# Three load buffers moved by 128 bytes in a decode step of attention plus a bilinear GLU

## The chip, the cores and the metric

The kernel runs on one core of a Trainium2 chip. The metric is the device time of one execution in microseconds (us). A core has TensorE (PE, matrix products), VectorE (DVE), ScalarE (ACT), GpSimd (POOL) and a queue engine (SP) that here issues all transfers; sixteen DMA engines carry them. The on-chip memory SBUF has 128 partitions, and a tile takes the same bytes in each of them. Place, in this document, means the byte within a partition at which a tile begins.

## The reference

One decode step for two sequences (B = 2), model width 512. The normalised input feeds an attention over the last 2048 positions of a cache with 32 heads of 128, and a gated product without a nonlinearity; both are added to the input. All values are 32-bit floats.

```python
xn = layernorm(x)                                   # x: (2, 1, 512)
q = (xn @ wq) as 32 heads of 128
k, v = k_cache[:, :, 6144:, :], v_cache[:, :, 6144:, :]      # W = max(256, 8192 // 4) = 2048
p = softmax(einsum("bhqd,bhkd->bhqk", q, k) * 128 ** -0.5)
A = einsum("bhqk,bhkd->bhqd", p, v) as (2, 1, 4096) @ wo
Bb = ((xn @ w_gate) * (xn @ w_up)) @ w_down         # hidden width 1376
return x + A + Bb
```

Nearly all bytes are those of k and v: 2 x 32 heads x 2048 x 128 x 4 bytes x 2 = 134 MB of the 159.5 MB that the kernel reads.

## The kernel before

**The stream.** The host lays all operands out in one array, `stream`, in the order in which they are used. `blocks()` (line 44) lists it as fields: for a head h, `("k", h, 4096)` and `("v", h, 4096)` floats in each partition, with slices of `wq` and `wo` of 512 floats beside them, and the weights of the GLU. Fields are grouped by three units of up to 4608 floats, so that a group fits one load buffer of `STEP` = 13,824 floats (55,296 bytes) in each partition.

**The loads.** `pump()` (lines 141 to 162) issues them on SP, each as one DMA of 128 contiguous rows, one for each partition. The first block (`x`, small selection matrices and a part of `wq`, 551 floats a partition) goes into a constant tile named `first`. All others go into three buffers, the pool `steps` (line 126): a buffer is taken when one is free, and `done()` (line 164) gives it back when the last of its fields has been used, and calls `pump()` again. There are 29 loads into these buffers: 16 of 55,296 bytes a partition, the others shorter; the last groups are cut into several loads of 2,048 to 18,432 bytes a partition so that the end of the stream can be used piece by piece.

**The work.** For each head, VectorE multiplies k in place by the broadcast q (`products`, line 272) and sums each product over the 128 of a row (`sums`, line 280). `maxima` and `weights` make the softmax with GpSimd's reductions across partitions and ScalarE's exponentials. TensorE weighs v by p (`weigh`, line 324), three heads behind k, brings the result into columns (`transpose`) and multiplies by `wo` (`project_o`). The GLU is done between the first heads. The order of the work on each engine is that of the text (`InOrder`, line 81, chains each instruction to the one before on its engine).

**Places.** The pools lie one behind the other in a partition: 16,512 bytes that are taken before the kernel's first tile, then the pool `const`, then `steps`, then `small`. In a pool tiles follow each other in the order in which they are first asked for, each rounded up to 32 bytes. The tiles of `const` are: `first` 2,204 bytes (2,208), `x_nat` 512, `mean_w` 512, `eps_t` 4 (32), six `p` of 512, four `oT` of 36 (64), `st`, `xc`, `sq` and `xn` of 32, `xnb` 4,096, `hT` 432 (448), `hX` 108 (128), `acc_sb` 2,048, `o_out` 512. That is 13,952, so `first` begins at 16,512 and the three buffers at 30,464, 85,760 and 141,056.

| tile | begins at byte | in units of 256 |
|---|---|---|
| `first` | 16,512 | 64.5 |
| load buffers | 30,464; 85,760; 141,056 | 119; 335; 551 |
| `s` (first of `small`) | 196,352 | 767 |

Every field of a load buffer is a multiple of 256 bytes wide (the narrowest are `wr` with 1,536 and the slices of `wq`, `wo` and `wd` with 2,048), so each field begins where its buffer does, modulo 256.

Of the kernel before, what the change touches and what calls it, by code (L numbers as in the profile page):

```python
# [8 lines left out]
F32 = mybir.dt.float32  # L9
# [7 lines left out]
P = 128  # L17
# [26 lines left out]
def blocks():  # L44

    def wd(n):
        return [("wd", i, D) for i in range(*WD[n])]

    def k(h):
        return [("k", h, CK)] + ([("wq", h, CP)] if h + HG < H else [])

    def v(h):
        return [("v", h, CK), ("wo", h, CO)]  # L60

    def gu(half):
        n = NC * (FH[half][1] - FH[half][0])
        return [("wg", half, n), ("wu", half, n)]

    units = []
    for h in range(LAG, H - 1):
        units += [k(h), v(h - LAG)]
    ones = [("pick", 0, 8 * B), ("rows", 0, NFB * B), ("carry", 0, M)]
    first = [("x", 0, B * NC)] + ones + [("w", 0, NC * DH)]  # L70
    loads = [[("w", 1, CQ - NC * DH)] + k(0) + k(1), gu(0) + k(2)]
    loads += [gu(1) + units[0] + units[1] + wd(0) + [("wr", 0, NS * P)]]
    loads += [sum(units[i : i + 3], []) for i in range(2, len(units), 3)]
    loads += [k(H - 1) + v(H - 1 - LAG) + wd(1)]
    out = [(("f", 0), first)] + [(("s", i), fields) for i, fields in enumerate(loads)]
    late, last = ("s", len(loads)), ("s", len(loads) + 1)
    out += [(late, v(H - 3)), (late, v(H - 2)), (last, [("v0", H - 1, CL)])]
    out += [(last, [("v1", H - 1, CK - CL)]), (last, [("wo", H - 1, CO)] + wd(2))]
    return out + [(last, wd(n)) for n in range(3, len(WD))]
# [33 lines left out]
def kernel(  # L113
# [11 lines left out]
    const = ctx.enter_context(tc.tile_pool(name="const", bufs=1))  # L125
# [3 lines left out]
    ps_c = ctx.enter_context(tc.tile_pool(name="ps_c", bufs=1, space=bass.MemoryType.PSUM))  # L129


    todo, at = [], 0
    for key, fields in blocks():
        todo.append((key, fields, at))
# [479 lines left out]
```

## Time and profile before

| | us |
|---|---|
| median of 3 runs (377.3 to 377.55) | 377.4 |
| the profiled execution | 377.5 |
| its span, first to last instruction | 375.7 |
| mean granted TensorE clock in it | 0.805 |

The page of the profile gives the busy time of each engine as a share of the span, then the span in 40 equal slices (a digit is the busy share in tenths; the row DMA is the mean over the sixteen DMA engines), then the DMA queues, and the chain of work that ended last. In the view of windows the last two columns are the DMA share and the GB/s moved. In the view of the DMA queues a packet is one row of a load, and the share is that of the sixteen engines' time in the window. In the view of waits the three numbers are the sum in us, how often, and the longest. In a tile's view the three durations are the least, the median and the greatest in ns. Nearly all instructions are recorded under line 97, the line of the helper that chains them, so tiles tell them apart.

### The profile page before, as it was taken

The numbers are of one execution on the slowest core, as the hardware profiler recorded it, in microseconds if no ns is written. First come the engines' busy times: TensorE is split into PE (matmuls) and PEld (weight loads), VectorE is DVE, ScalarE is ACT, GpSimd is POOL, SyncE is SP. The second block draws the span as 40 slices with busy tenths as digits, with TensorE's granted clock in tenths as the row PEclk, the third lists the DMA queues.
The fourth block names the chain that finished last, engine by engine and source line by source line (L and its number), as shares of the span: only waits on it lengthen the run. The fifth ranks groups of instructions, "written<-read, shape, count | busy, mean of one in ns | idle before, by whom it ended". The sixth has DMA issues, their size and how long they took to land.

```text
span 375.7 us, 2858 instructions
## 1 busy us (share of the span) xinstructions
PE 254.2 (68%) x1084; PEld 88.5 (24%) x1084; DVE 294.1 (78%) x146; ACT 58.6 (16%) x259; POOL 25.3 (7%) x78
## 2 busy tenths in 40 slices
PE   3496497886547486854858476685846669637996
PEld 3241023331112122211212121231212122212334
DVE  3299691998599499769949976994996799599950
ACT  1021001122021111201112020211202011211131
POOL 1001000000000000100000100000000000000010
PEclk9998967998697666888768696885869676857999
DMA  8999999899999999999999999999999999999995
GB/s 346 445 436 454 426 408 471 383 465 449 395 466 406 442 455 400 459 418 436 460 400 449 424 430 459 402 442 430 430 459 406 437 444 436 419 431 443 398 421 221
DMA packets 4492, 159.70 MB, mean 425 GB/s; under 512 B 512, under 2 KB 640, under 8 KB 1152
## 3 DMA queue, kind: packets, MB, share of 16 engines
q1 hardware_dynamic: 4480, 159.54, 98.5%
q8 instruction: 8, 0.13, 0.1%
q14 instruction: 4, 0.03, 0.0%
HBM read 159.48 MB, written 0.06 MB: 425 GB/s over the span
## 4 chain that ended last, share of the span: by engine, by line
DMA 63%; DVE 26%; PE 8%; ACT 1%; issue 0%; SPq 0%; DVEq 0%
DMA step<-in_stream_dram 63%; DVE s L97 13%; DVE step L97 13%; PE o_ps L97 3%; PE q L97 2%; PE acc L97 2%; PE tr L97 1%; ACT o_sb L97 0%; DVE m L97 0%; ACT oT L97 0%; SPq L97 0%; DVE rec L97 0%; DVE o_out L97 0%; DVEq L97 0%
## 5 line engine op out<-in xcount | busy, mean ns | idle before, releaser
L97 DVE TENSOR_TENSOR step<-step,q 128x4096 f32<-128x4096 f32 x31 | 136.6, 4407 | 52.4 <-DMA step<-in_stream_dram 52.4
L97 PE MATMUL q<-step,xnb 128*128 128x512 f32 (+1 forms) x128 | 92.4, 872 | 76.4 <-DMA step<-in_stream_dram 76.4
L97 DVE TENSOR_REDUCE s<-step 128x32 f32<-128x4096 f32 x32 | 141.4, 4419 | 1.1
L97 PE MATMUL o_ps<-step,p 128*16 128x512 f32 x512 | 68.9, 672 | 11.5 <-DMA step<-in_stream_dram 11.5
L97 PEld LDWEIGHTS q<-step,xnb 128*128 128x128 f32 x128 | 32.3, 275 | 130.5 <-DMA step<-in_stream_dram 77.5
L97 PE MATMUL acc<-step,oT 128*9 128x512 f32 (+1 forms) x88 | 35.4, 552 | 9.3 <-ACT oT L97 8.1
L97 PE MATMUL tr<-first,o_sb 128*128 128x2 f32 (+2 forms) x198 | 28.1, 261 | 15.4 <-ACT o_sb L97 13.0
L97 ACT COPY o_sb<-o_ps 128x512 f32<-128x512 f32 (+1 forms) x25 | 14.1, 568 | 140.7 <-PE o_ps L97 140.7
L97 PEld LDWEIGHTS tr<-first,o_sb 128*128 128x128 f32 x198 | 26.0, 200 | 36.8 <-ACT o_sb L97 32.4
L290 POOL PARTITION_ALL_REDUCE mm<-m x32 | 11.3, 354 | 283.1 <-DVE rec L97 180.1
L97 PEld LDWEIGHTS o_ps<-step,p 128*16 128x16 f32 x512 | 13.4, 104 | 69.9 <-issue 54.4
L97 ACT ACTIVATE nm<-mm 128x2 f32<-128x2 f32 x32 | 6.5, 203 | 131.4 <-POOL mm L290 131.4
L97 ACT ACTIVATE p<-s,nm 128x16 f32<-128x16 f32 x64 | 19.2, 300 | 1.0
L97 ACT ACTIVATE oT<-tr,rec 128x1 f32<-128x1 f32 x64 | 12.2, 260 | 28.5 <-PE tr L97 28.5
L306 POOL PARTITION_ALL_REDUCE sum<-rs x32 | 12.7, 398 | 55.0 <-ACT p L97 55.0
L97 PE MATMUL o_ps<-step,xn 128*2 128x512 f32 (+1 forms) x48 | 13.9, 616 | 0.0
L97 ACT ACTIVATION_READ_ACCUMULATOR p<-s,nm 128x1 f32 x64 | 12.0, 187 | 0.0
L97 DVE TENSOR_TENSOR step<-step,tr 128x4096 f32<-128x4096 f32 x1 | 4.4, 4422 | 9.3 <-DMA step<-in_stream_dram 9.3
L97 PEld LDWEIGHTS acc<-step,oT 128*9 128x9 f32 x88 | 4.5, 91 | 19.4 <-ACT oT L97 12.7
L97 PE MATMUL q<-xnb,mean_w 128*128 128x512 f32 (+2 forms) x18 | 8.3, 551 | 0.0
L97 DVE TENSOR_TENSOR o_out<-acc,x_nat 128x128 f32<-128x128 f32 x1 | 0.3, 292 | 8.8 <-PE acc L97 8.8
L97 DVE TENSOR_REDUCE m<-s 128x2 f32<-128x32 f32 x32 | 5.9, 186 | 1.1
(39 smaller groups left out, 40.5 us busy)
## 6 DMA issues: line engine op xcount, KB each, us to landing
step<-in_stream_dram SPq DMA_DIRECT2D x16, 6912.0 KB, 31.1
step<-in_stream_dram SPq DMA_DIRECT2D x2, 6400.0 KB, 32.8
step<-in_stream_dram SPq DMA_DIRECT2D x1, 6720.0 KB, 45.4
step<-in_stream_dram SPq DMA_DIRECT2D x1, 6656.0 KB, 29.0
step<-in_stream_dram SPq DMA_DIRECT2D x1, 5376.0 KB, 15.3
step<-in_stream_dram SPq DMA_DIRECT2D x1, 4864.0 KB, 29.6
step<-in_stream_dram SPq DMA_DIRECT2D x2, 2304.0 KB, 17.1
step<-in_stream_dram SPq DMA_DIRECT2D x1, 1536.0 KB, 14.6
```

The costliest lines, as they stand in the source:

```text
L97: made = call(*args, **kwargs)
L290: nc.gpsimd.partition_all_reduce(mm, m, P, bass_isa.ReduceOp.max)
L306: nc.gpsimd.partition_all_reduce(sum_t[h], rs, P, bass_isa.ReduceOp.add)
```

## The change

A tile of 32 floats in each partition, 128 bytes, is asked for in the pool `const` before any other. Nothing writes or reads it.

```diff
     ps_c = ctx.enter_context(tc.tile_pool(name="ps_c", bufs=1, space=bass.MemoryType.PSUM))
 
 
+
+    const.tile([P, 32], F32, name="place")
     todo, at = [], 0
     for key, fields in blocks():
```

All tiles of `const` behind it, the three load buffers and the tiles of `small` begin 128 bytes later: `first` at 16,640 (65 x 256), the buffers at 30,592, 85,888 and 141,184 (119.5, 335.5 and 551.5 x 256). The size of a buffer, the loads, their order and all instructions stay.

## The prediction

> **What bounds the kernel now.** I read the page from the top: busy times, the slices, the DMA queues, the chain that ended last. Then the windows of two stretches, the waits of VectorE and of the load queue, and the view of the DMA queues in three short windows.
>
> ```profile
> span 375.7 us, 2858 instructions
> ...
> PE 254.2 (68%) x1084; PEld 88.5 (24%) x1084; DVE 294.1 (78%) x146; ACT 58.6 (16%) x259; POOL 25.3 (7%) x78
> ...
> DMA  8999999899999999999999999999999999999995
> ...
> q1 hardware_dynamic: 4480, 159.54, 98.5%
> ...
> DMA 63%; DVE 26%; PE 8%; ACT 1%; issue 0%; SPq 0%; DVEq 0%
> ```
>
> No engine is busy for more than 78% of the span, but the queue that carries the loads keeps all sixteen DMA engines at work for 98.5% of it; the idle rest is the first slice and the last. The chain names loads for 63% and VectorE for 26%. That share of VectorE needs a second look, since work on the chain need not be what limits:
>
> ```profile
> core 0: us, PE busy (x) PEld busy (x) DVE busy (x) ACT busy (x) POOL busy (x), PEclk, DMA share, GB/s
> 100.00:200.00 100.00, 65.69 (x252) 20.31 (x255) 83.49 (x37) 14.95 (x69) 6.77 (x18) 0.76 1.00 434
> 1.70:372.10 370.40, 253.43 (x1072) 88.26 (x1076) 292.99 (x142) 57.60 (x259) 24.16 (x67) 0.80 1.00 431
> ```
>
> ```profile
> DVE step L97 <- DMA step<-in_stream_dram: 61.7, 11, 9.3
> ...
> SPq L97 <- DVE s L97: 309.8, 21, 31.4
> ```
>
> In the middle of the run (100 to 200 us) the DMA engines have no idle time (share 1.00, 434 GB/s) while VectorE rests for 16.5 us in 100 and waits for loads 61.7 us in all. The load queue (SP) in turn waits for VectorE's sums 309.8 us, but that is a queue waiting for a free buffer with its two earlier loads still under way:
>
> ```profile
> step<-in_stream_dram SPq DMA_DIRECT2D x16, 6912.0 KB, 31.1
> ```
>
> A load of 6912 KB (7.08 MB) takes 16.3 us at 434 GB/s and lands 31.1 us after its issue. So it stands 31.1 - 16.3 = 14.8 us behind the load ahead of it, and an issue that came late by less than that would leave no hole in the stream. Where the stream begins and ends, two windows in slices show, 0 to 3 us (75 ns a slice) and 371 to 372.4 us (35 ns a slice):
>
> ```profile
> GB/s 0 0 0 0 0 0 0 0 0 0 0 0 0 0 0 0 0 0 0 0 0 0 29 147 59 118 88 147 206 147 147 235 323 323 353 441 2014 3102 147 1809
> ```
>
> ```profile
> GB/s 351 293 176 176 176 468 117 59 351 176 176 117 293 176 234 234 176 176 176 117 117 234 117 117 59 59 117 0 0 59 0 0 0 0 0 0 0 0 0 0
> ```
>
> The first bytes move after 22 empty slices, at 1.7 us, the last in the 30th slice, at 372.05. The time is therefore: start (1.7 us), 370.4 us of unbroken stream, and 3.6 us for what follows the last bytes.
>
> **The change, part by part.** It adds no instruction: a tile that nothing writes or reads has no memset, no DMA and no wait. It removes none, and the order on each engine and on each queue (SP's and GpSimd's among them) is that of before. What moves is places. From the tile sizes the constants end and the first load buffer begins at byte 30,464 of a partition, which is 119 x 256; a buffer is 55,296 = 216 x 256 bytes, so all three begin on even multiples of 128, and every field in them is a multiple of 256 wide. With 128 bytes ahead the buffers begin at 119.5 x 256, and every row of every one of their 29 loads starts and ends in the middle of a 256-byte piece. The constants and the small tiles move by 128 as well.
>
> *Term 1: the rows of the loads.* A load writes 128 rows, one in each partition, and sixteen engines share them: 29 x 128 / 16 = 232 rows on each engine. What a row costs follows from two windows. In the last loads the rows are 2,048 bytes; the long loads' rows are 55,296 bytes:
>
> ```profile
> DMA packets 51, 0.09 MB, mean 188 GB/s; under 512 B 6, under 2 KB 6, under 8 KB 51
> ...
> q1 hardware_dynamic: 51, 0.09, 48.9%
> ```
>
> ```profile
> DMA packets 883, 43.39 MB, mean 434 GB/s; under 512 B 96, under 2 KB 96, under 8 KB 96
> ...
> q1 hardware_dynamic: 880, 43.35, 100.2%
> ```
>
> The first (371.3 to 371.8 us) moves 188 GB/s in 48.9% of its time, so 384.5 GB/s while busy, or 16 x 2048 / 384.5 = 85.2 ns for a row. The second (100 to 200 us) gives 434 / 1.002 = 433.1 GB/s, or 2042.8 ns for a row. The difference over 53,248 bytes is 0.0368 ns a byte: 4.7 ns for 128 bytes, 9.4 ns for 256, and 85.2 - 75.3 = 9.9 ns for a row whatever its length.
>
> Is a start on an odd multiple of 128 dearer? The trace of before has one load of that sort. The tile `first` begins at 16,512 = 64.5 x 256, and its 128 rows of 2,204 bytes are the first on the engines. Here are two windows in which nothing else moves, 2.3 to 2.7 us and 2.4 to 2.6 us:
>
> ```profile
> DMA packets 58, 0.13 MB, mean 320 GB/s; under 512 B 0, under 2 KB 0, under 8 KB 58
> ...
> q1 hardware_dynamic: 58, 0.13, 83.0%
> ```
>
> ```profile
> DMA packets 31, 0.07 MB, mean 342 GB/s; under 512 B 0, under 2 KB 0, under 8 KB 31
> ...
> q1 hardware_dynamic: 31, 0.07, 90.2%
> ```
>
> While busy: 320 / 0.830 = 385.5 GB/s and 342 / 0.902 = 379.2. By the fit an undisturbed row of 2,204 bytes takes 9.9 + 81.0 = 90.9 ns, which is 387.9 GB/s. With 128 bytes' time more it would be 368.9, with 256 bytes' more 351.6. The two readings lie by the first of these, 0.6% and 2.2% under it. So I take 0 for this term. Its ends: upward, one more 256-byte piece on each row, 232 x 9.4 = 2.2 us, as the cost that belongs to a row's two ends; and where a cost goes with the bytes, the lower reading's 2.2% of 370.4 us = 8.3 us. Downward, what the even places could be costing now is at most the fixed 9.9 ns of a row, 232 x 9.9 = 2.3 us: nothing else in a stream at share 1.00 can be won, because bytes over the steady rate is all that is left. The zero is nearest to the rows of `first`, which have the place in question; their weakness is that they are short, few, and run while the stream is only starting.
>
> [...]
>
> *Term 2: VectorE and TensorE on the moved buffers.* Both read the buffers, VectorE writes its products back into them, and all these operands now start 128 bytes on.
>
> ```profile
> L97 DVE TENSOR_TENSOR step<-step,q x31: 4398/4400/4422, 25.6 to 352.4; 128x4096 f32<-128x4096 f32 x31
> ...
> L97 PE MATMUL o_ps<-step,p x512: 592/592/1062, 62.8 to 368.6; 128*16 128x512 f32 x171
> ```
>
> The 31 products take 4398 to 4422 ns in whichever of the three buffers, on all the field offsets that occur. No row shows them on an odd multiple of 128; I take 0. This would be covered in any case up to a point: VectorE has 83.49 us of work in the 100, so its work could grow by a fifth before it took the place of the loads. TensorE at 65.69 has more room. Without that cover, 1% on VectorE's 294.1 us would cost 2.9 us. The ends of this term are therefore 0 and 0, except in the tail after the last bytes, where a few matmuls read the buffer: below 0.1 us.
>
> *Term 3: the moved small tiles and constants.*
>
> ```profile
> first<-in_stream_dram SPq DMA_DIRECT2D x1, 275.5 KB, 2.9
> ```
>
> `first` moves to 65 x 256; its load lands 2.9 us after issue, ahead of the longest of VectorE's waits for a long load (9.3 us, the row above), so a few ns there are hidden. The sum of all is 0.
>
> The profiled execution took 377.5 us, span 375.7 and 1.8 around it; the median of the three runs is 377.4, so I put the sum against the median: 377.4 + 0 = 377.4 us.
>
> **The rivals.** *Rows pay at their ends* (slower). The mechanism of term 1: each of the 232 rows on an engine gets one piece more, partly empty. Price 1.1 us (128 bytes) to 2.2 us (256 bytes): 378.5 to 379.6 us. It decides at once, since nothing hides a longer stream: from 0.75 us / 232 = 3.2 ns a row it is measurable. For it: the stream has no slack. Against it: the two windows of `first`, and the second of them not strongly. [...]
>
> *Every 256-byte piece pays* (slower). If source pieces land across two destination pieces all along the row, the cost goes with the bytes. The lower reading of `first` allows 2.2%, so up to 377.4 + 8.3 = 385.7 us. A whole eighth of a piece's time (1.18 ns on 9.4) would be 46 us and would have shown in `first` as 347 GB/s; that one I rule out.
>
> *The odd places are better* (faster). If part of the 9.9 ns of a row comes from where it begins, up to 2.3 us go: 375.1 to 376.6 us. For it: the fit has such a fixed part. Against: rows of `first`, on an odd multiple, show the same fixed part within the reading, and the engines have no idle time to win back.
>
> *Nothing moves*, because an untouched tile gets no room: 377.4 us, the forecast's time by another way.
>
> *The engines slow down* by over a fifth on such operands and VectorE becomes the bound: from 83.49 x 1.2 = 100 in 100 us on, each further 1% about 3 us. No row speaks for it.
>
> **How the numbers follow.** Between no change and a small one the line is 0.2%, 0.75 us, about what a measurement of this kernel can tell from no change. No change (nothing moving included): 0.48. Rows pay at their ends: 0.22. Every piece pays: 0.10. Engines: 0.04. Better: 0.16. That gives faster 0.16, same 0.48, slower 0.36, and the time of the likeliest, 377.4. The range goes down to 375.6, most of the faster case, and up to 380.2, past the ends' 379.6 and into the lower part of the case of every piece; about 0.05 stays out below and 0.12 above. The forecast's own range is 376.7 to 378.1.
>
> **What the profile after would show.** If right: the same instruction counts, share 1.00 and 434 GB/s between 100 and 200 us, the products at 4400 ns, and the last bytes at about 372.1 us. If rows pay: the same shape, but 433.4 or less in that window, the end of the stream 1 to 2 us later, and VectorE waiting longer for loads by the same amount. If every piece pays: 424 to 433 GB/s there. If the odd places are better: over 434 at the same share. In all of these the short rows show it most: the last loads' 2-KB rows at other than 384.5 GB/s while busy, and `first`, now on an even multiple, away from 380. What would make the prediction wrong is a cost or a gain of the write side that only a full stream shows, which the short start of `first` can't.

## The result and the profile after

The changed kernel takes 378.44 us (median of 7 runs, 378.17 to 379.39) where the one before takes 377.40 (7 runs, 377.30 to 377.62): 1.0027 times as long, 95% interval 1.0018 to 1.0036. That is 1.04 us more, past the 0.2% that I had set as the line to no change, and above the forecast's own range of 376.7 to 378.1 us.

The profiled execution after took 378.54 us, with a span of 376.7 where before had 375.7. These are the lines of its page that answer to those quoted of before:

```profile
span 376.7 us, 2858 instructions
...
PE 255.8 (68%) x1084; PEld 88.2 (23%) x1084; DVE 294.1 (78%) x146; ACT 58.6 (16%) x259; POOL 25.3 (7%) x78
...
q1 hardware_dynamic: 4480, 159.54, 98.4%
...
DMA 63%; DVE 17%; PE 17%; ACT 2%; issue 1%; SPq 1%; DVEq 0%
...
step<-in_stream_dram SPq DMA_DIRECT2D x16, 6912.0 KB, 31.1
```

The instruction counts, VectorE's 294.1 us, the packets and the bytes are the same. The chain names TensorE more (17%, before 8%) and VectorE less (17%, before 26%), with the loads' share unchanged at 63%; the time that VectorE and TensorE stand there for passes under a full stream (share 1.00 in both, from 1.7 us to 372.1 before and to 373 after). VectorE's products on the moved buffers, and its waits, in the views of the tile and of the waits:

```profile
L97 DVE TENSOR_TENSOR step<-step,q x31: 4398/4401/4422, 25.8 to 353.0; 128x4096 f32<-128x4096 f32 x31
```

```profile
DVE step L97 <- DMA step<-in_stream_dram: 63.0, 11, 9.5
```

The products cost what they did (4400 ns before). VectorE waits for loads 63.0 us instead of 61.7, 1.3 us more in the same 11 waits. So the loads are late, and not an engine. The stream itself, between 100 and 200 us, and its end, from 371 to 373.4 us in slices of 60 ns:

```profile
DMA packets 880, 43.22 MB, mean 432 GB/s; under 512 B 96, under 2 KB 96, under 8 KB 96
...
q1 hardware_dynamic: 877, 43.19, 100.0%
```

```profile
GB/s 239 410 239 341 307 171 444 205 307 171 239 307 171 171 341 273 239 239 239 239 273 171 137 171 103 68 34 68 68 34 0 34 34 0 0 0 0 0 0 0
```

The DMA engines are as full as before (share 1.00) and move 432 / 1.000 = 432.0 GB/s where before they moved 433.1. The view rounds to whole GB/s, so this is rough; by the bytes it is 43.19 / 1.000 MB against 43.35 / 1.002, 0.2% less. The end of the stream is the firmer figure: the last bytes move in the 33rd slice, at 373.0 us, where before it was 372.05. Nearly the whole loss is thus a stream that ends 0.9 us later, which on 370.4 us is 0.25%.

### The profile page after: what moved, and what is told of

Same layout as the page of the kernel before. It is cut to its first block, busy times and chain, and to the rows that moved or that the text cites. A ratio compares the mean times of both kernels' runs of the same rounds, so it can differ in the third digit from the quotient of the medians.

```text
span 376.7 us, 2858 instructions
## 1 busy us (share of the span) xinstructions
PE 255.8 (68%) x1084; PEld 88.2 (23%) x1084; DVE 294.1 (78%) x146; ACT 58.6 (16%) x259; POOL 25.3 (7%) x78
## 4 chain that ended last, share of the span: by engine, by line
DMA 63%; DVE 17%; PE 17%; ACT 2%; issue 1%; SPq 1%; DVEq 0%
DMA step<-in_stream_dram 63%; DVE s L97 8%; DVE step L97 8%; PE o_ps L97 6%; PE q L97 4%; PE acc L97 4%; PE tr L97 2%; ACT o_sb L97 1%; SPq L97 1%; ACT oT L97 1%; DVE m L97 0%; ACT hT L97 0%; DVE o_sb L97 0%; ACT hX L97 0%; DVE o_out L97 0%
## 5 line engine op out<-in xcount | busy, mean ns | idle before, releaser
L97 PE MATMUL o_ps<-step,p 128*16 128x512 f32 x512 | 71.9, 697 | 11.9 <-DMA step<-in_stream_dram 11.8
L97 PE MATMUL acc<-step,oT 128*9 128x512 f32 (+1 forms) x88 | 33.8, 533 | 9.3 <-ACT oT L97 8.1
L97 PE MATMUL o_ps<-step,xn 128*2 128x512 f32 (+1 forms) x48 | 12.2, 553 | 0.0
L97 PE MATMUL acc<-step,hT 128*9 128x128 f32 (+2 forms) x58 | 7.8, 354 | 0.1
```

Source lines behind the costliest of these rows:

```text
L97: made = call(*args, **kwargs)
```

## The experiments

Theory A: a row pays once where it begins (and ends) off a multiple of 256 bytes in SBUF. Theory B: the same loss goes with the bytes. Theory C: the moved constants and small tiles, or just any other placing, cost it. Each run was timed in five rounds beside the kernel before on the same chip (377.40 to 377.44 us).

### Which of the moved things it is

**Everything by 256 instead of 128.**

```diff
-    const.tile([P, 32], F32, name="place")
+    const.tile([P, 64], F32, name="place")
```

> The unused tile is made 256 bytes, so that everything moves by twice as much and the load buffers begin on even multiples of 128 again (30,720 = 120 x 256). Theory A, a row pays where it begins or ends inside a 256-byte piece: no cost, 377.4 us, ratio 1.000. Theory C, the moved constants and small tiles cost the time, or merely any other placing than that of before: about 378.4 us, ratio 1.0027.

Measured: 377.46 us, 1.0001 (0.9993 to 1.0010).

**The buffers and what is behind them, not the constants.** Against before:

```diff
     o_out = const.tile([P, P], F32, name="o_out")
+    const.tile([P, 32], F32, name="behind")
```

> The unused tile of 128 bytes stands behind all other constants, so that the constants keep their places and the load buffers (and the small tiles behind them) move by 128 bytes. Theory A: 378.4 us, ratio 1.0027, all of the loss. Theory C in the form that the constants (first among them) cost it: 377.4 us, ratio 1.000.

Measured: 378.34 us, 1.0025 (1.0016 to 1.0035).

**The constants by 128, the buffers by 256.** The changed kernel with the line `behind` of the run above as well.

> One unused tile of 128 bytes ahead of the constants and one behind them: the constants move by 128 bytes as in the changed kernel, the load buffers by 256, back on an even multiple. Theory A: 377.4 us, ratio 1.000. Theory C in the form of the constants: 378.4 us, ratio 1.0027.

Measured: 377.51 us, 1.0002 (0.9993 to 1.0011).

Theory C falls. Moving constants by 128 (1.0002), or everything by 256 (1.0001), costs nothing that can be measured, and moving what stands behind the constants by 128 costs all of it (1.0025 of 1.0027). In the window from 100 to 200 us the first and the second of these runs look like this:

```profile
DMA packets 882, 43.29 MB, mean 433 GB/s; under 512 B 96, under 2 KB 96, under 8 KB 96
...
q1 hardware_dynamic: 878, 43.24, 99.9%
```

```profile
DMA packets 880, 43.18 MB, mean 432 GB/s; under 512 B 96, under 2 KB 96, under 8 KB 96
...
q1 hardware_dynamic: 876, 43.13, 99.8%
```

While busy that is 433 / 0.999 = 433.4 and 432 / 0.998 = 432.9 GB/s, too coarse to tell the places apart. The trace also has the time of each single row, and that tells them apart. Of the 2048 rows of 55,296 bytes, so many took 2041 or 2042 ns:

| kernel | rows at 2041 or 2042 ns | mean of all 2048, ns |
|---|---|---|
| before | 1926 | 2044.2 |
| everything by 256 | 1923 | 2043.5 |
| constants by 128, buffers by 256 | 1924 | 2043.8 |
| the change | 914 | 2046.8 |
| buffers by 128, constants in place | 845 | 2047.0 |

These runs also give the unit. Before, the buffers begin 256 bytes behind a multiple of 512, in the first and the third run on a multiple of 512, and both places cost the same (377.40 us against 377.46 and 377.51). It is 256 that counts, not 512. The small tiles move with the buffers in all of these, so in the second run they aren't told apart by their place; that it is the loads' rows follows from the table above and from the next section but one.

### The price against the offset

The unused tile was made 32, 64, 96, 192 and 224 bytes (8, 16, 24, 48 and 56 floats in the line of the diff).

> The unused tile is 32 bytes: the load buffers begin 32 bytes behind a multiple of 256. Theory A with the price by the part of the piece that lies ahead of the row (a quarter of the part at 128 bytes): 1.04 / 4 = 0.26 us, 377.7 us, ratio 1.0007. Theory A with one price for any start that isn't on a multiple of 256: 378.4 us, ratio 1.0027. If 32 bytes are dearer than 128 because of a finer unit, above 1.0027.

> The unused tile is 224 bytes: the load buffers begin 224 bytes behind a multiple of 256. One price for any start off a multiple of 256, as the run at 32 bytes speaks for: 378.4 to 378.7 us, ratio 1.0027 to 1.0032. A price by the part of the piece ahead of the row: 1.04 x 224 / 128 = 1.8 us, 379.2 us, ratio 1.0048. A price by the bytes up to the next boundary (large at 32, small at 224): 377.7 us, ratio 1.0007.

> The unused tile is 64 bytes. One price for any start off a multiple of 256, between what was measured at 128 and at 32 and 224 bytes: 378.3 to 378.7 us, without a pattern. Theory D, a row pays one fixed part for a start off 256 and a further part when its ends aren't multiples of 64: as at 128 bytes, 378.3 us, ratio 1.0025.

> The unused tile is 96 bytes, no multiple of 64. Theory D: as at 32 and 224 bytes, 378.7 us, ratio 1.0033. If the further cost at 32 and 224 comes from the nearness of the boundary and not from 64: as at 128 bytes, 378.3 us, ratio 1.0025.

> The unused tile is 192 bytes, a multiple of 64 beyond 128. Theory D: 378.3 us, ratio 1.0025. A price that grows with the part of the piece ahead of the row: 1.04 x 192 / 128 = 1.56 us, 379.0 us, ratio 1.0041.

| bytes behind a multiple of 256 | us | ratio | 95% interval |
|---|---|---|---|
| 0 (moved by 256) | 377.46 | 1.0001 | 0.9993 to 1.0010 |
| 32 | 378.73 | 1.0032 | 1.0020 to 1.0045 |
| 64 | 378.57 | 1.0029 | 1.0017 to 1.0040 |
| 96 | 378.36 | 1.0023 | 1.0013 to 1.0032 |
| 128 (the change) | 378.44 | 1.0027 | 1.0018 to 1.0036 |
| 192 | 378.47 | 1.0027 | 1.0015 to 1.0038 |
| 224 | 378.67 | 1.0033 | 1.0020 to 1.0045 |

It is about one price for all six places off a multiple of 256: 0.9 to 1.3 us. A price that grows with the part of the piece ahead of the row would be 1.0007 at 32 and 1.0048 at 224, and both lie outside what was measured. A price by the bytes up to the next boundary, expected at 1.0007 at 224, falls as well. Theory D, a further cost where the ends aren't multiples of 64, expected 96 at 1.0033 and 64 at 1.0025; it came out the other way round, so D isn't borne out. Whether 32 and 224 are a little dearer than the rest stays open, since all these intervals overlap. One trace of each points that way: the recorded times of all packets of the load queue add up to 370.98 and 370.93 us an engine at 32 and 224, to 370.5 to 370.8 at the other places off a multiple of 256, and to 369.9 to 370.0 on one.

### The reading side

In SBUF nothing moves; the array of the loads begins with 32 unused floats, so all rows of the load buffers are read from 128 bytes behind a multiple of 256, if the array itself begins on one, which is not on record. In the second run the changed kernel's tile is there as well.

```diff
-    todo, at = [], 0
+    todo, at = [], 32
...
-        "stream": np.concatenate(parts),
+        "stream": np.concatenate([np.zeros(32, a.dtype)] + parts),
```

> The places in SBUF are those of before; the array of the loads begins with 128 unused bytes, so that each row is read from an odd multiple of 128 and written to an even one. Theory A for the writing side alone: 377.4 us, ratio 1.000. Theory A for the reading side as well: 378.4 us, ratio 1.0027. If what counts is only that source and destination lie differently in their 256-byte pieces: 378.4 us too, and the run with both moved, at 377.4, then tells this apart.

> The changed kernel's places in SBUF and 128 unused bytes ahead of the array of the loads: rows are read from and written to odd multiples of 128. Theory A for the writing side alone: 378.4 us, ratio 1.0027. Theory of the unlike positions: 377.4 us, ratio 1.000. Both sides paying one after the other: 379.5 us, ratio 1.0055.

Measured: 377.55 us, 1.0003 (0.9994 to 1.0012), for the source alone; 378.26 us, 1.0024 (1.0014 to 1.0033), for both. Moving the place that is read by 128 bytes costs nothing here, and a like offset on both sides doesn't help. The price goes with the place that is written. What these two runs can't exclude is that the array begins off a multiple of 256, so that a price of reading was paid in all kernels alike.

### By the row or by the byte

Each of the 22 long loads is issued in four parts of a quarter of the columns, cut at multiples of 256 bytes; once on the places of before, once on those of the changed kernel.

```diff
-            sp.dma_start(tiles[key][:, c0:c1], src)
+            n = 4 if c1 - c0 >= 9728 else 1
+            cut = [(c1 - c0) * i // n // 64 * 64 for i in range(n)] + [c1 - c0]
+            for lo, hi in zip(cut, cut[1:]):
+                sp.dma_start(tiles[key][:, c0 + lo : c0 + hi], src[:, lo:hi])
```

> Each of the 22 loads of 38,912 bytes a partition or more is issued as four loads of a quarter of the columns, on the places of before: 760 rows on an engine in place of 232, the same bytes. All theories: dearer than before by 528 rows at the 5 to 10 ns of a row whatever its length, 2.6 to 5.3 us, 380.0 to 382.7 us. It is the base of the next run.

> The same four parts a load, with the places of the changed kernel. Theory A (each row pays, whatever its length): above the run on even places by 760 x 4.5 ns = 3.4 us. Theory B (the cost goes with the bytes, 0.27% of the stream): above it by 1.0 us, as in the kernels with long rows.

Measured: 380.41 us (380.25 to 380.59) on the even places, 383.63 us (383.54 to 383.75) on the odd ones. The odd places now cost 3.22 us where they cost 1.04 with the long rows. Divided by the rows of an engine that is 3.22 us / 760 = 4.2 ns a row against 1.04 us / 232 = 4.5 ns a row: the same price a row, with more than three times the rows and the same bytes. Theory B, which expected 1.0 us, falls. Here the rate shows it too, even places first, 100 to 200 us:

```profile
DMA packets 3508, 43.03 MB, mean 430 GB/s; under 512 B 395, under 2 KB 395, under 8 KB 395
...
q1 hardware_dynamic: 3504, 42.98, 100.6%
```

```profile
DMA packets 3472, 42.68 MB, mean 427 GB/s; under 512 B 384, under 2 KB 384, under 8 KB 384
...
q1 hardware_dynamic: 3468, 42.63, 100.6%
```

At the same share of 100.6%, 430 GB/s fall to 427. The recorded rows agree: of the 8192 rows of 13,824 bytes, 8173 took 516 ns on the even places and 1573 on the odd ones, and their mean rose from 516.6 to 521.0 ns. This also answers a rival that the times alone leave, a price by the load: each load has eight rows on an engine, so the two quotients would come out alike. But on the odd places 6619 of the 8192 rows took longer than 516 ns, and not one in eight.

And more than three times as many rows on even places cost 380.41 - 377.44 = 2.97 us / 528 = 5.6 ns for a row whatever its length (the further loads' packets of under 512 bytes included: 512 in the run before, 1568 with the parts), a little more than the 4.2 to 4.5 that a start off 256 adds to it.

## Why the prediction was wrong

**What bounds the kernel** was read rightly: an unbroken stream of loads with nothing under which a longer stream could hide. All of the loss arrived in the time, 1.04 us in the runs and 0.9 us in the end of the stream.

**Term 1 failed**, the rows of the loads, at the step "So I take 0 for this term". The bracket above it was right: the rival of rows that pay at their ends priced 1.1 us for half a piece and 2.2 for a whole one on 232 rows, and 1.04 us was measured in place of the 0, 4.5 ns a row. What misled was the row that I let decide, the two windows of `first`, 379.2 and 385.5 GB/s while busy on an odd multiple of 128. The lower of them lay midway between 387.9 (no price) and 368.9 (half a piece), and not by the first. After the change `first` stands on an even one, so the same two windows (2.3 to 2.7 and 2.4 to 2.6 us) show whether they can tell the places apart:

```profile
DMA packets 48, 0.11 MB, mean 264 GB/s; under 512 B 0, under 2 KB 0, under 8 KB 48
...
q1 hardware_dynamic: 48, 0.11, 69.3%
```

```profile
DMA packets 23, 0.05 MB, mean 253 GB/s; under 512 B 0, under 2 KB 0, under 8 KB 23
...
q1 hardware_dynamic: 23, 0.05, 65.1%
```

They read 264 / 0.693 = 381.0 and 253 / 0.651 = 388.6 GB/s, on average 0.6% above the odd place's, where 4.5 ns on 91 would be 5%. The recorded times say the same: the median of the 128 rows of `first` is 89 ns on either place. Nor do the last 2-KB rows show it, of which I had said that they would show it most: from 372.2 to 372.6 us the changed kernel moves them at 380.3 GB/s while busy against 384.5 before, 1.1% less where 4.5 ns on 85 would be 5%:

```profile
DMA packets 34, 0.06 MB, mean 143 GB/s; under 512 B 7, under 2 KB 7, under 8 KB 34
...
q1 hardware_dynamic: 34, 0.06, 37.6%
```

So next to nothing of the price is in the recorded time of these short rows that run with gaps between them (shares 38% to 90% here). It shows where the engines are full: the rows of 12,288 and of 18,432 bytes took 460.0 and 686.0 ns on average before, and 464.2 and 689.8 after. I had named that weakness ("only a full stream shows"), and let the zero stand against it. Even in the full stream the records hold only a part: all packets of an engine add up to 370.0 us before and 370.6 after, 0.6 of the 1.04 us. Why it is so was not tried.

The lower price of the rival of rows that pay at their ends, an estimated 1.1 us for 128 bytes' time on each row (232 x 4.7 ns, from the two windows of before), was near the 1.04 us in sum. A price by the bytes isn't what the runs show: on the writing side it doesn't grow with the bytes between the multiple of 256 and the row (1.0032 at 32 bytes, 1.0027 at 128, 1.0033 at 224), and moving the source by 128 bytes cost nothing (1.0003). So that the estimate came near at 128 bytes is in part luck.

**Term 2**, the engines on the moved buffers, held: VectorE's products took 4401 ns against 4400, its work 294.1 us against 294.1, and TensorE's products of p and v 592 ns at the median against 592. **Term 3** held: the constants moved by 128, with the buffers on an even place, cost nothing (1.0002).

**The rivals.** Rows that pay at their ends is what happened (4.5 ns a row); at which end isn't shown, since every row of these loads is a multiple of 256 bytes long and so begins and ends at the same offset. Nor is it shown that a row gets one piece more: that was the author's picture, and the runs show the price alone. Every piece pays is excluded by the four parts, where the same bytes cost 3.22 us. The odd places being better, nothing moving, and slower engines are excluded by the result and by term 2.

## What to carry to other kernels

Where a full stream of loads sets the time, let each row of a load begin in SBUF on a multiple of 256 bytes (all rows here are multiples of it long); here a row off it cost its engine 4.2 to 4.5 ns on average at an offset of 128, with rows of up to 55,296 bytes as with rows of up to 18,432, so it matters more where rows are short and many (3.22 us with 760 rows on an engine, 1.04 with 232). How far down that goes is open: at the end of the stream rows of 4,096 bytes took 161.1 ns on average after against 159.0 before, and rows of 2,048 bytes 84.4 against 84.0, and no full stream of such rows was tried. A small tile ahead in the same partition is enough to move all buffers behind it (128 bytes here, for 1.04 us). And a price read from transfers that run with gaps says little of the price in a full stream (the two places of `first` read 0.6% apart here, where 4.5 ns would be 5%): look for the row in the same state as the work that it is to stand for.

## What was not expected of the hardware

A write off a multiple of 256 bytes costs one price a row (0.9 to 1.3 us on 232 rows, 4.0 to 5.7 ns) at 32, 64, 96, 128, 192 and 224 bytes alike, about half of the 9.4 ns that 256 bytes take by the prediction's two windows, while moving the source by 128 bytes costs nothing. In the traces it is not spread evenly: of the 2048 rows of 55,296 bytes, 1926 took 2041 or 2042 ns before and 914 after, while those of 2046 to 2055 ns grew from 60 to 916:

```
rows of 55,296 bytes, by the recorded ns    before   after
2041 to 2042                                  1926     914
2043 to 2045                                    28     202
2046 to 2048                                    35     570
2049 to 2055                                    25     346
over 2055                                       34      16
```

At other offsets 259 and 266 of these rows (32 and 224 bytes), 767 and 496 (64 and 192) and 965 (96) took 2041 or 2042 ns. In one trace each, the pattern thus seems to go with the distance to the nearer multiple of 256, much as the times did at 32 and 224. What makes the price stays open.
